# Attention with a gated MLP and a spectral MLP on one core: order of the state scan, the key product and the transposes, and masks read from PSUM

## The chip, the cores and the metric

One core of a Trainium2 chip runs one program. The engines are TensorE (PE; its weight loads are the rows PEld), VectorE (DVE), ScalarE (ACT), GpSimd (POOL) and SyncE (SP, which here only issues transfers). The metric is device time in microseconds (us) of one launch, lower is better; a run of the kernel before and one of the kernel after are compared by their medians.

## The reference

Three blocks follow each other; all of it is fp32.

```
# 1 linear attention with decay: q, k, v, alpha are [4, 8, 768, 48]
for t in range(768):
    state = alpha[:, :, t, :, None] * state + einsum('bhd,bhe->bhde', k[:, :, t], v[:, :, t])
    y[:, :, t] = einsum('bhd,bhde->bhe', q[:, :, t], state)
# 2 gated MLP on x = y as [4, 768, 384]
u, v = split(gelu(x @ w_in), 2)              # d_ff 1024
v = layernorm(v) * g_ln
x = x + (u * (w_sg @ v + b_sg)) @ w_out      # w_sg is [768, 768], over the sequence
# 3 spectral MLP
u = x + real(fft(fft(x, axis=1), axis=2))
out = u + relu(layernorm(u) @ w_ch1) @ w_ch2 # 384 -> 1536 -> 384
```

## The kernel before

**Attention (`attention`, L53 to L295).** The 32 heads are 16 pairs (NG), two heads on 2 x 48 partitions. The sequence is cut into 6 chunks of 128. A pair is a "full step", a half of it (3 chunks) a "half-step" `h`; `g, f = divmod(h, 2)`. Per pair DVE does a backward scan of alpha (`scan1`, L104), a clamp and a reciprocal (L107, L108), the forward scan (`scan2`, L113), the key product (L114, k times the backward scan, in place) and the state scan over chunks (`zscan`, L146). POOL makes the query product (L123). PE makes scores (L154), DVE masks them (L159), and PE makes the output from scores and values (L167, L168) and from queries and states (L173); ACT copies it out (L178 to L181). The keys are transposed by PE (L129), copied by ACT (L131), and multiplied with the values (L141, L142) into the PSUM tile `kp`. Behind `kp`'s 288 columns, in the same tile, lies one column `one` of ones, which both scans read by broadcast. ACT also checks the range of alpha (L119).

**The order.** Every engine does its instructions in the order in which the program writes them; semaphores are set by the framework from the tiles that an instruction reads and writes. The half-steps 2 to 31 are a loop (L263 to L294). An even one starts with `scan1(g + 2)` and then `zscan(g)`, an odd one with `scan2(g + 2)`, which holds the key product, and the query product. Then come scores and mask of the next half-step, one projection unit (`fill(h, 0)`, from half-step 10 on), the transposes (`trk`) of the next pair, the output (`pv`), and at odd half-steps both halves of the key-value product of the next pair (`kv`). Last stands `fill(h, 1)`, two steps of the weight conversion.

**Weight conversion (`Wide`, L419 to L466).** The weights come in as 64-bit numbers. 62 jobs of 128 x 256 or 128 x 192 turn them into fp32 pieces: DVE masks the high word (L438), ACT rescales (L439 to L441), DVE joins sign and body (L446), masks again (L447), and POOL adds and multiplies the low parts (L445, L448, L449). `first` and `second` are the two steps of a job; a third action, `done`, splits the result into a high and a low part (ACT, then POOL, L385 and L388) or stores it. Two steps per half-step convert the input weights and 6 others in the attention, to half-step 20; two of them are `second` of one job and `first` of the next.

**Gated MLP (`gmlp`, L636 to L746).** `proj` runs projection units (L588 to L609) with normalization on DVE and ACT in between, and after each unit two steps of `wsg` (the split of the spatial weight; its low part by POOL or DVE) and one of the weight conversion. `spatial(b)` has 8 units: 18 matmuls with the spatial weight into PSUM, DVE's L700 and L701, ACT's copy L704, DVE's subtraction L707, then the output product `wout` of the unit before, and three conversion steps. `wo_ready` converts ahead of the first four `wout` whatever output weight pieces are still missing.

Of the kernel before, what the change touches and what calls it, by code (L numbers as in the profile page):

```python
# [22 lines left out]
NC = S // CH  # L23
# [29 lines left out]
def attention(tc, st):  # L53
# [22 lines left out]
    qhs = [const(f"qh{i}", [R2, NC, CE]) for i in range(3)]  # L76
    bank = ps_t.tile([R2, 512], F32, name="kp")
    kp, one = bank[:, 0:D * NC].rearrange("p (e c) -> p e c", c=NC), bank[:, D * NC:D * NC + 1]
    ps_u = ctx.enter_context(tc.tile_pool(name="a_psu", bufs=1, space=PSUM, reuse_waits="tile"))
# [21 lines left out]
    def scan1(g, cs=ALL):  # L101
        ak, sf = G[g]["ak"], sfs[g % 3]
        a, z = cs.start * CE, cs.stop * CE
        V.tensor_tensor_scan(out=flat(sf)[:, a:z - 1][:, ::-1], data0=ak[:, a + 2:z + 1][:, ::-1], data1=one.to_broadcast([R2, z - a - 1]), initial=1.0, op0=ALU.mult, op1=ALU.min)  # L104
        V.memset(grid(ak)[:, cs, 0], 0.0)
        p0 = w_p.tile([R2, NC], F32, tag="p0", name="p0")[:, cs]
        V.tensor_scalar(out=p0, in0=sf[:, cs, 0], scalar1=1e-14, scalar2=None, op0=ALU.max)  # L107
        V.reciprocal(out=grid(ak)[:, cs, 1], in_=p0)  # L108

    def scan2(g, cs=ALL):  # L110
        ak, sf, rr = G[g]["ak"], sfs[g % 3], qhs[g % 3]
        j = slice(cs.start * CE, cs.stop * CE)
        V.tensor_tensor_scan(out=flat(rr)[:, j], data0=ak[:, j], data1=one.to_broadcast([R2, j.stop - j.start]), initial=0.0, op0=ALU.mult, op1=ALU.max)  # L113
        V.tensor_tensor(out=sf[:, cs, 1:CE - 1], in0=chunks(ak[:, QK:QK + S])[:, cs], in1=sf[:, cs, 1:CE - 1], op=ALU.mult)  # L114

# [99 lines left out]
    V.memset(kp, 0.0)  # L215
    V.memset(one, 1.0)
    warmup(4)
    NH = 2 * NG
    half = slice(0, 3), slice(3, NC)

    def ready(g, f):
        scan1(g, half[f])
        scan2(g, half[f])
        qhat(g, half[f])

# [31 lines left out]
    scan1(2)  # L257
    zscan(1)
    scan2(2)
    qhat(2)  # L260
    acheck(2)
    load_ak(5)
    for h in range(2, NH):  # L263
        g, f = divmod(h, 2)
        nx, ahead, near = h + 1 < NH, g + 2 < NG, g + 1 < NG
        if ahead and not f:
            load_v(g + 2)
            scan1(g + 2)
            if h > 2:
                zscan(g)  # L270
        if ahead and f:
            scan2(g + 2)
            qhat(g + 2)
            acheck(g + 2)
            if g + 5 < NG:
                load_ak(g + 5)
        if not (ahead or f):
            zscan(g)
        if nx:
            for i in range(3):  # L280
                sc(h + 1, i)
            att(h + 1)
            st["fill"](h, 0)
        if near and h > 2:
            trk(g + 1, f)
        pv(h)
        if h == 2:
            trk(2, 0)
        if near and f:
            kv(g + 1, 0)  # L290
            kv(g + 1, 1)
        if h == NH - 3:
            flag(tc, st, ones[:, 0:2], w_p, ps_t)
        st["fill"](h, 1)  # L294
    ctx.close()  # L295
# [122 lines left out]

class Wide:  # L419
    def __init__(self, nc, pool, w, const, ahead):  # L420
        self.nc, self.pool, self.w, self.const, self.ahead = nc, pool, w, const, ahead
        self.n_done = 0

    def tile(self, n, dt, w, bufs):
        return self.pool.tile([128, self.w], dt, tag=n, name=n, bufs=bufs)[:, 0:w]

    def load(self, job):
# [5 lines left out]
    def first(self, j):  # L433
# [3 lines left out]
        low = j["low"] = j["raw"].bitcast(F32).rearrange("p (a b) -> p a b", b=2)[:, :, 0]  # L437
        nc.vector.tensor_scalar(out=x, in0=j["hi"], scalar1=0x7FFF0000, scalar2=None, op0=ALU.bitwise_and)  # L438
        nc.scalar.activation(mid, h16[:, :, 2], AF.Copy, scale=2.0 ** -20)  # L439
# [3 lines left out]
    def second(self, j):  # L443
        nc, x, mid, hi = self.nc, j["x"], j["mid"], j["hi"]
        nc.gpsimd.tensor_tensor(out=mid, in0=mid, in1=j["low"], op=ALU.add)  # L445
        nc.vector.scalar_tensor_tensor(out=x, in0=hi, scalar=-2 ** 31, in1=x, op0=ALU.bitwise_and, op1=ALU.bitwise_or)  # L446
        nc.vector.tensor_scalar(out=hi, in0=x, scalar1=-2 ** 23, scalar2=None, op0=ALU.bitwise_and)  # L447
        nc.gpsimd.tensor_tensor(out=mid, in0=mid, in1=hi.bitcast(F32), op=ALU.mult)  # L448
# [187 lines left out]
def gmlp(tc, st):  # L636
# [33 lines left out]

    def proj(units, b, n):
        ns = norm(b)
        for i, u in enumerate(units):
            u()
            if i == 1:
                flush()
            take(ns, 1 + (i >= len(units) - n))
            st["gfill"](-1, 1)
        pj.flush()
        for _ in ns:  # L680
            pass
# [7 lines left out]
    def spatial(b):  # L689
        ut = pj.u[b % 2]  # L690
        for h in range(2):
            acc = [None] * KD
            for d in range(KH):
# [30 lines left out]
                if b < 2 and t < NT:  # L724
                    src = st["x"][b + 2][:, t]
                    A.copy(xh[:, t], src)
                    xlag.append(lambda t=t, src=src: V.tensor_tensor(out=xl[:, t], in0=src, in1=xh[:, t].bitcast(F32), op=ALU.subtract))
                st["gfill"](h, 3)
                if b == B - 1:
                    st["fft"](KH * h + d)  # L730

    for _ in pj.early:
        pass
    proj(us(1), 0, 0)
    st["after_u"](0)
    rp = ctx.enter_context(tc.tile_pool(name="g_r", bufs=2, **kw))
    spatial(0)
    proj(vs(2) + us(2), 1, 0)
    spatial(1)
    proj(vs(3), 2, 1)  # L740
    spatial(2)
    proj(us(3), 3, 0)
    st["after_u"](B - 1)
# [340 lines left out]
def network(tc, st, tag, front):  # L1084
# [10 lines left out]
    wd = Wide(nc, pool(in_u, "wide", "left"), WJ, st["bias"], 2)  # L1095
    F = {}
    st["proj"] = Proj(tc, st, pool(in_u, "pj", "left"))
    F["wsg"] = plain_steps(nc, pool(raw, "stg1", "left", 4), wsg_jobs(nc, st), 4, HT)
# [142 lines left out]
```

## Time and profile before

| | |
|---|---|
| three runs | 823.48, 824.86, 825.70 us; median 824.86 |
| the profiled execution | 824.26 us, of which the span shown is 822.5 |
| mean granted clock of TensorE | 0.939 of 2.4 GHz |
| busy, share of the span | PE 763.0 us (93%), PEld 708.5 (86%), DVE 518.2 (63%), ACT 319.8 (39%), POOL 263.9 (32%) |
| stages | attention to 206 us, then the gated MLP, then the spectral MLP |

Shares over the whole span mix stages with different limits; a stage is read by itself. "Clock" is the granted share of full speed: 1.00 is 2.4 GHz, 0.50 is 1.2 GHz. A matmul of fp32 operands appears as more than one PE instruction, so that one pair's key-value product of 10 matmuls is 20 rows. In the timeline a bracket gives the idle time of the engine ahead of an instruction and what ended it.

### The profile page before, as it was taken

What the parts mean: (1) busy time and instruction counts of PE and PEld (TensorE: products, weight loads), DVE (VectorE), ACT (ScalarE), POOL (GpSimd) and SP (SyncE); (2) the same over time, 40 slices, a digit from 0 to 9 for tenths busy, and PEclk for the clock granted to TensorE, in tenths of its full rate; (3) what the DMA queues carried; (4) which work ended last, traced back from release to release, by engine and by line L of the source; (5) the groups of instructions that cost most, each with busy time, mean ns of one, the idle gap of its engine ahead of it and who ended that gap; (6) DMA issues with size and microseconds to landing.
All of it is one profiled execution on the core that took longest, in us unless ns stands there. A gap on an engine that the chain in (4) does not pass through costs nothing.

```text
span 822.5 us, 13577 instructions
## 1 busy us (share of the span) xinstructions
PE 763.0 (93%) x5077; PEld 708.5 (86%) x5077; DVE 518.2 (63%) x1163; ACT 319.8 (39%) x757; POOL 263.9 (32%) x309
## 2 busy tenths in 40 slices
PE   6878888999788989979999999999999999999996
PEld 4656667887787879869999999999999999999996
DVE  6778898875788888886667776327533354424321
ACT  3546565553754464452333435123222222122210
POOL 2356774531587566544033266003000000000000
PEclk7755798999989999989999999999999999999998
DMA  9985758733513333310022032000000000000001
GB/s 232 197 173 127 170 121 189 168 76 71 138 58 90 94 92 100 88 49 29 1 60 59 9 109 77 29 1 30 2 29 2 30 1 1 30 1 29 21 9 33
DMA packets 43597, 58.08 MB, mean 71 GB/s; under 512 B 5473, under 2 KB 34177, under 8 KB 43521
## 3 DMA queue, kind: packets, MB, share of 16 engines
q1 hardware_dynamic: 42944, 56.85, 27.6%
q8 instruction: 42, 0.69, 0.4%
q14 instruction: 35, 0.28, 0.1%
q10 hardware_dynamic: 576, 0.26, 0.1%
HBM read 42.93 MB, written 9.44 MB: 64 GB/s over the span
## 4 chain that ended last, share of the span: by engine, by line


## 5 line engine op out<-in xcount | busy, mean ns | idle before, releaser
L1012 DVE SCALAR_TENSOR_TENSOR hl<-h,hh 128x384 fp32r<-128x384 f32 x96 | 53.4, 556 | 143.3 <-ACT hh L1011 143.2
L1011 ACT ACTIVATE hh<-h 128x384 fp32r<-128x384 f32 x96 | 47.2, 491 | 177.3 <-PE h L416 177.3
L414 PE MATMUL h<-unh,wc 128*128 128x384 f32 x288 | 99.3, 345 | 0.0
L415 PE MATMUL h<-unl,wc 128*128 128x384 f32 x288 | 96.4, 335 | 0.1
L416 PE MATMUL a<-wc,hl 128*128 128x384 f32 x288 | 96.4, 335 | 0.0
L416 PE MATMUL h<-unh,wc 128*128 128x384 f32 x288 | 96.3, 334 | 0.0
L415 PE MATMUL a<-wc,hh 128*128 128x384 f32 x288 | 96.2, 334 | 0.0
L414 PE MATMUL a<-wc,hh 128*128 128x384 f32 x288 | 96.2, 334 | 0.0
L416 PE MATMUL h<-wsg,vl 128*128 128x384 f32 x192 | 66.8, 348 | 5.7 <-DVE vl L668 5.7
L415 PE MATMUL h<-wsg,vh 128*128 128x384 f32 x192 | 66.7, 347 | 4.4 <-POOL wsg L388 4.3
L414 PE MATMUL h<-wsg,vh 128*128 128x384 f32 x192 | 66.7, 347 | 1.4 <-ACT ut L609 1.4
L448 POOL TENSOR_TENSOR wm<-wm,wr 128x192 f32<-128x192 f32 (+1 forms) x62 | 43.0, 694 | 44.4 <-DVE wr L447 42.1
L445 POOL TENSOR_TENSOR wm<-wm,wr 128x192 f32<-128x192 f32 (+1 forms) x62 | 46.5, 750 | 28.1 <-ACT wr L440 28.1
L415 PEld LDWEIGHTS h<-unl,wc 128*128 128x128 f32 x288 | 54.2, 188 | 0.3 <-DVE unl L388 0.3
L416 PEld LDWEIGHTS a<-wc,hl 128*128 128x128 f32 x288 | 54.1, 188 | 0.1
L414 PEld LDWEIGHTS h<-unh,wc 128*128 128x128 f32 x288 | 54.1, 188 | 0.0
L416 PEld LDWEIGHTS h<-unh,wc 128*128 128x128 f32 x288 | 54.1, 188 | 0.0
L414 PEld LDWEIGHTS a<-wc,hh 128*128 128x128 f32 x288 | 54.1, 188 | 0.0
L415 PEld LDWEIGHTS a<-wc,hh 128*128 128x128 f32 x288 | 54.1, 188 | 0.0
L173 PE MATMUL y<-qh,z 48*48 48x128 f32 x320 | 30.6, 329 | 20.9 <-DVE z L146 20.9
L449 POOL TENSOR_TENSOR wm<-wx,wm 128x192 f32<-128x192 f32 (+1 forms) x62 | 47.4, 765 | 4.9
L123 POOL TENSOR_TENSOR qh<-q,qh 112x768 f32<-112x768 f32 (+1 forms) x18 | 37.2, 2068 | 34.2 <-DVE qh L113 26.2
(213 smaller groups left out, 1953.1 us busy)
## 6 DMA issues: line engine op xcount, KB each, us to landing
ak<-in_qa SPq DMA_DIRECT2D x26, 290.4 KB, 4.9
v<-in_v SPq DMA_DIRECT2D x16, 288.0 KB, 4.3
wr<-in_w_d SPq DMA_DIRECT2D x18, 256.0 KB, 2.7
wr<-in_w_d SPq DMA_DIRECT2D x24, 192.0 KB, 2.4
raw<-w_s SPq DMA_DIRECT2D x12, 384.0 KB, 3.2
out<-o SPq DMA_DIRECT2D x24, 192.0 KB, 1.9
q<-in_qa SPq DMA_DIRECT2D x26, 144.0 KB, 5.2
wr<-in_win_d SPq DMA_DIRECT2D x12, 256.0 KB, 4.3
```

The source lines that it names most:

```text
L123: P.tensor_tensor(out=qh, in0=chunks(G[g]["q"])[:, cs], in1=qh, op=ALU.mult)
L173: T.matmul(y[e, i, :], d["z"][e, :, c], qhs[g % 3][e, c, 2:], start=False, stop=True, skip_group_check=True)
L414: T.matmul(out, lh, rh, start=first, stop=False)
L415: T.matmul(out, lh, rl, start=False, stop=False)
L416: T.matmul(out, ll, rh, start=False, stop=last)
L445: nc.gpsimd.tensor_tensor(out=mid, in0=mid, in1=j["low"], op=ALU.add)
L448: nc.gpsimd.tensor_tensor(out=mid, in0=mid, in1=hi.bitcast(F32), op=ALU.mult)
L449: nc.gpsimd.tensor_tensor(out=mid, in0=x.bitcast(F32), in1=mid, op=ALU.add)
L1011: A.activation(hh, p, AF.Relu)
L1012: V.scalar_tensor_tensor(out=hl, in0=p, scalar=0.0, in1=hh.bitcast(F32), op0=ALU.max, op1=ALU.subtract)
```

## The change

The tile `kp` becomes 128 partitions high, and three constant columns join `one` in it: the clamp's bound (1e-14) and the two bit masks. The clamp and, while the attention runs, the masks of the conversion become two-operand instructions that read these columns by broadcast. The key product leaves `scan2` and is issued ahead of its forward scan. The state scan is issued ahead of the backward scan. Transposes come ahead of the projection unit; behind them stand the conversion steps, the unit and the output. The key-value product is issued one half per half-step. In the gated MLP the conversion steps are spread differently: none in the first projection, three and four in turn in the spatial stage.

```diff
@@ -74,8 +74,9 @@
...
     qhs = [const(f"qh{i}", [R2, NC, CE]) for i in range(3)]
-    bank = ps_t.tile([R2, 512], F32, name="kp")
-    kp, one = bank[:, 0:D * NC].rearrange("p (e c) -> p e c", c=NC), bank[:, D * NC:D * NC + 1]
+    full = ps_t.tile([128, 512], F32, name="kp")
+    bank, masks = full[0:R2], [full[:, D * NC + 2 + i:D * NC + 3 + i].bitcast(I32) for i in range(2)]
+    kp, one, tiny = bank[:, 0:D * NC].rearrange("p (e c) -> p e c", c=NC), bank[:, D * NC:D * NC + 1], bank[:, D * NC + 1:D * NC + 2]
     ps_u = ctx.enter_context(tc.tile_pool(name="a_psu", bufs=1, space=PSUM, reuse_waits="tile"))
...
@@ -104,14 +105,17 @@
...
         p0 = w_p.tile([R2, NC], F32, tag="p0", name="p0")[:, cs]
-        V.tensor_scalar(out=p0, in0=sf[:, cs, 0], scalar1=1e-14, scalar2=None, op0=ALU.max)
+        V.tensor_tensor(out=p0, in0=sf[:, cs, 0], in1=tiny.to_broadcast(list(p0.shape)), op=ALU.max)
         V.reciprocal(out=grid(ak)[:, cs, 1], in_=p0)
...
     def scan2(g, cs=ALL):
-        ak, sf, rr = G[g]["ak"], sfs[g % 3], qhs[g % 3]
+        ak, rr = G[g]["ak"], qhs[g % 3]
         j = slice(cs.start * CE, cs.stop * CE)
         V.tensor_tensor_scan(out=flat(rr)[:, j], data0=ak[:, j], data1=one.to_broadcast([R2, j.stop - j.start]), initial=0.0, op0=ALU.mult, op1=ALU.max)
-        V.tensor_tensor(out=sf[:, cs, 1:CE - 1], in0=chunks(ak[:, QK:QK + S])[:, cs], in1=sf[:, cs, 1:CE - 1], op=ALU.mult)
+
+    def khat(g, cs=ALL):
+        ak, sf = G[g]["ak"], sfs[g % 3][:, cs, 1:CE - 1]
+        V.tensor_tensor(out=sf, in0=chunks(ak[:, QK:QK + S])[:, cs], in1=sf, op=ALU.mult)
 
...
@@ -214,6 +218,10 @@
...
     V.memset(one, 1.0)
+    V.memset(tiny, 1e-14)
+    for m, z in zip(masks, Wide.MASKS):
+        V.memset(m, z)
+    st["wide"].masks = masks
     warmup(4)
...
@@ -221,6 +229,7 @@
...
         scan2(g, half[f])
+        khat(g, half[f])
         qhat(g, half[f])
...
@@ -256,6 +265,7 @@
...
     zscan(1)
+    khat(2)
     scan2(2)
...
@@ -265,10 +275,11 @@
...
             load_v(g + 2)
-            scan1(g + 2)
             if h > 2:
                 zscan(g)
+            scan1(g + 2)
         if ahead and f:
+            khat(g + 2)
             scan2(g + 2)
...
@@ -280,18 +291,18 @@
...
             att(h + 1)
-            st["fill"](h, 0)
         if near and h > 2:
             trk(g + 1, f)
+        st["fill"](h, 1)
+        st["fill"](h, 0)
         pv(h)
...
             trk(2, 0)
-        if near and f:
-            kv(g + 1, 0)
-            kv(g + 1, 1)
+        if near:
+            kv(g + 1, f)
         if h == NH - 3:
             flag(tc, st, ones[:, 0:2], w_p, ps_t)
-        st["fill"](h, 1)
+    st["wide"].masks = None
     ctx.close()
...
@@ -417,12 +428,20 @@
...
 class Wide:
+    MASKS = 0x7FFF0000, -2 ** 23
+
     def __init__(self, nc, pool, w, const, ahead):
         self.nc, self.pool, self.w, self.const, self.ahead = nc, pool, w, const, ahead
-        self.n_done = 0
+        self.n_done, self.masks = 0, None
 
...
         return self.pool.tile([128, self.w], dt, tag=n, name=n, bufs=bufs)[:, 0:w]
+
+    def mask(self, out, x, i):
+        if self.masks is None:
+            self.nc.vector.tensor_scalar(out=out, in0=x, scalar1=self.MASKS[i], scalar2=None, op0=ALU.bitwise_and)
+        else:
+            self.nc.vector.tensor_tensor(out=out, in0=x, in1=self.masks[i].to_broadcast(list(x.shape)), op=ALU.bitwise_and)
 
...
@@ -435,7 +454,7 @@
...
         low = j["low"] = j["raw"].bitcast(F32).rearrange("p (a b) -> p a b", b=2)[:, :, 0]
-        nc.vector.tensor_scalar(out=x, in0=j["hi"], scalar1=0x7FFF0000, scalar2=None, op0=ALU.bitwise_and)
+        self.mask(x, j["hi"], 0)
         nc.scalar.activation(mid, h16[:, :, 2], AF.Copy, scale=2.0 ** -20)
...
@@ -444,7 +463,7 @@
...
         nc.vector.scalar_tensor_tensor(out=x, in0=hi, scalar=-2 ** 31, in1=x, op0=ALU.bitwise_and, op1=ALU.bitwise_or)
-        nc.vector.tensor_scalar(out=hi, in0=x, scalar1=-2 ** 23, scalar2=None, op0=ALU.bitwise_and)
+        self.mask(hi, x, 1)
         nc.gpsimd.tensor_tensor(out=mid, in0=mid, in1=hi.bitcast(F32), op=ALU.mult)
...
@@ -668,14 +687,14 @@
...
 
-    def proj(units, b, n):
+    def proj(units, b, n, c):
         ns = norm(b)
...
             take(ns, 1 + (i >= len(units) - n))
-            st["gfill"](-1, 1)
+            st["gfill"](-1, c)
         pj.flush()
...
@@ -725,21 +744,21 @@
...
                     xlag.append(lambda t=t, src=src: V.tensor_tensor(out=xl[:, t], in0=src, in1=xh[:, t].bitcast(F32), op=ALU.subtract))
-                st["gfill"](h, 3)
+                st["gfill"](h, 3 + d % 2)
                 if b == B - 1:
...
         pass
-    proj(us(1), 0, 0)
+    proj(us(1), 0, 0, 0)
     st["after_u"](0)
...
     spatial(0)
-    proj(vs(2) + us(2), 1, 0)
+    proj(vs(2) + us(2), 1, 0, 1)
     spatial(1)
-    proj(vs(3), 2, 1)
+    proj(vs(3), 2, 1, 1)
     spatial(2)
-    proj(us(3), 3, 0)
+    proj(us(3), 3, 0, 1)
     st["after_u"](B - 1)
...
@@ -1094,6 +1113,7 @@
...
     F = {}
+    st["wide"] = wd
     st["proj"] = Proj(tc, st, pool(in_u, "pj", "left"))
...
     first, second, spill = win_jobs(nc, st), wo_jobs(nc, st), spill_jobs(nc, st)
```

## Rows read from the trace of the kernel before

**Rows 1.** Busy time by stage: length, engines with counts, clock, DMA share, GB/s.

```profile
58.00:71.60 13.60, 11.21 (x93) 8.61 (x93) 11.16 (x16) 7.09 (x18) 8.22 (x9) 0.50 0.71 151
...
152.20:206.00 53.80, 53.05 (x587) 43.51 (x588) 37.43 (x66) 27.79 (x67) 16.82 (x13) 1.00 0.41 94
206.00:231.00 25.00, 18.00 (x91) 16.27 (x91) 18.55 (x27) 16.87 (x43) 15.24 (x17) 0.93 0.46 122
...
250.00:282.00 32.00, 27.50 (x142) 24.68 (x141) 27.66 (x56) 11.93 (x30) 22.17 (x26) 1.00 0.36 104
...
400.00:800.00 400.00, 399.85 (x2411) 391.97 (x2410) 199.71 (x575) 116.05 (x255) 54.28 (x58) 1.00 0.09 27
```

**Rows 2.** DVE groups, 30 to 155.1 us: busy, mean ns, idle before.

```profile
L104 DVE TENSOR_TENSOR_SCAN sf<-ak,kp 112x779 f32<-112x779 f32 x10 | 17.7, 1765 | 0.0
...
L447 DVE TENSOR_SCALAR wr<-wx 128x256 int32<-128x256 int32 x18 | 10.9, 606 | 0.6
L438 DVE TENSOR_SCALAR wx<-wr 128x256 int32<-128x256 int32 x18 | 10.3, 570 | 0.0
L446 DVE SCALAR_TENSOR_TENSOR wx<-wr,wx 128x256 int32<-128x256 int32 x18 | 8.4, 464 | 17.5 <-ACT wx L441 17.5
```

**Rows 3.** Single lines, min/median/max ns; then L107's total from 30 to 155.1.

```profile
L438 DVE TENSOR_SCALAR wx<-wr x62: 245/280/1077, 33.8 to 377.0; 128x192 int32<-128x192 int32 x32, 128x256 int32<-128x256 int32 x30
...
L159 DVE TENSOR_TENSOR at<-sp,mask x32: 917/944/958, 9.5 to 199.9; 128x768 f32<-128x768 f32 x32
...
L107 DVE TENSOR_SCALAR p<-sf x18: 161/162/523, 4.7 to 179.6; 112x6 f32<-112x6 f32 x14, 112x3 f32<-112x3 f32 x4
...
30.00:155.10 125.10, 3.69 (x10) 0.75 0.75 162
```

**Rows 4.** DVE's timeline in one full step: start us, length us.

```profile
72.46 0.28 DVE L438 TENSOR_SCALAR wx<-wr 128x256 int32<-128x256 int32 x1
74.46 0.42 DVE L446 SCALAR_TENSOR_TENSOR wx<-wr,wx 128x256 int32<-128x256 int32 x1 [1.71 <-ACT wx L441]
...
77.29 1.43 DVE L114 TENSOR_TENSOR sf<-ak,sf 112x768 f32<-112x768 f32 x1
...
79.51 0.90 DVE L438 TENSOR_SCALAR wx<-wr 128x256 int32<-128x256 int32 x1
80.99 0.42 DVE L446 SCALAR_TENSOR_TENSOR wx<-wr,wx 128x256 int32<-128x256 int32 x1 [0.58 <-ACT wx L441]
...
83.94 0.52 DVE L107 TENSOR_SCALAR p<-sf 112x6 f32<-112x6 f32 x1
```

**Rows 5.** POOL's timeline in the same full step.

```profile
77.86 2.40 POOL L123 TENSOR_TENSOR qh<-q,qh 112x768 f32<-112x768 f32 x1
```

**Rows 6.** ACT's timeline in the same full step.

```profile
72.90 0.48 ACT L178 COPY ys<-y 112x384 f32<-112x384 f32 x1 [4.52 <-PE y L173]
...
73.93 0.50 ACT L441 ACTIVATE wx<-wx,bias 128x256 int32<-128x256 int32 x1
```

**Rows 7.** PE's timeline in the same full step.

```profile
71.75 1.10 PE L173 MATMUL y<-qh,z 48*48 48x128 f32 x8 [2.38 <-DVE z L146]
...
77.86 0.34 PE L141 MATMUL kp<-v,kt 128*64 128x48 f32 x1
...
79.09 1.23 PE L154 MATMUL sp<-qh,sf 48*128 48x128 f32 x8
```

**Rows 8.** Waits, 0 to 210 us: total, times, longest.

```profile
DVE sf L104 <- PE kp L142: 8.8, 3, 3.8
```

**Rows 9.** PE's timeline in the first spatial unit, and POOL's.

```profile
227.54 0.69 PE L415 MATMUL h<-wsg,vh 128*128 128x384 f32 x1 [3.21 <-POOL wsg L388]
...
229.95 0.69 PE L415 MATMUL h<-wsg,vh 128*128 128x384 f32 x1 [1.07 <-POOL wsg L388]
...
226.38 4.50 POOL L388 TENSOR_TENSOR wsg<-raw,wsg 128x384 fp32r<-128x384 f32 x4
```

**Rows 10.** DVE's timeline in the first spatial stage: the start of two units.

```profile
237.29 0.61 DVE L700 SCALAR_TENSOR_TENSOR t<-h,gt,bb 128x384 f32<-128x384 f32 x1
...
243.20 0.60 DVE L700 SCALAR_TENSOR_TENSOR t<-h,gt,bb 128x384 f32<-128x384 f32 x1
```

## The prediction

> **What bounds the kernel now.** I read the busy time by stage first. From 400 to 800 us TensorE (PE) is busy 399.85 of 400 us at full clock, so whatever is gained or lost before 400 us goes whole into the end [rows 1]. The linear attention fills the first 206 us. Its last part, from 152.2 to 206, is PE's again (53.05 of 53.80 us). Between about 30 and 152 PE is not the limit: in the 13.60 us from 58.0 to 71.6 it is busy 11.21 us at a clock of 0.50 (1.2 GHz), and VectorE (DVE) 11.16 us. Which of them sets the pace is read from the DVE groups of 30 to 155.1: the scans, the masks and the products have 0.0 to 0.6 us of idle time ahead of them, and the only DVE instruction that waits is L446, 17.5 us in 18 times, for ScalarE's (ACT) L441 [rows 2]. So DVE paces the attention up to 155 us, by its busy time and by this one wait.
>
> The busy time is longer than the work. L438, a mask of 256 columns, takes 245 ns at least, 1077 at most, and 570 in the mean of this stretch [rows 2, 3]. The timeline shows when: at 79.51 it takes 0.90 us, and GpSimd (POOL) is in its 2.40 us product from 77.86 to 80.26; at 72.46 with POOL idle it takes 0.28 [rows 4, 5]. The clamp L107 goes the same way, 0.16 alone and 0.52 at 83.94 [rows 3, 4]. An instruction with one operand in PSUM does not: L159 stays between 917 and 958 ns in all 32 places [rows 3].
>
> The wait of L446 has a floor of 0.58 us (L438, then L441, then L446 follow each other), seen at 80.99, and is 1.71 in the even half-steps, as at 74.46 [rows 4]. There ACT stood 4.52 us at the copy L178, in front of L441 in its queue, until PE had finished the state products L173; these had waited for the state scan L146, which DVE does only behind the backward scan L104 [rows 6, 7].
>
> **The change part by part, over the 18 jobs of 256 columns in this stretch.**
>
> Masks. 36 instructions take 10.9 + 10.3 = 21.2 us [rows 2]. With the mask read from PSUM the instruction becomes a two-operand one that the trace of before does not have. Bounds: 0.28, as the free mask at 72.46, and 0.90, as the hindered one at 79.51 [rows 4]. I take 0.42, the free L446, which has the same width and two operands. 36 x 0.42 = 15.1, saves 6.1 us. At 0.28 it would save 11.1, at 0.60 (no cure at all) nothing.
>
> The Trainium skill has a rule against this part. In "VectorE: DVE Perf Modes", section "The perf-mode tier table", an fp32 `tensor_scalar` in SBUF runs at 2x and a `tensor_tensor`, or anything with PSUM, at 1x. By that table alone each mask would go from 0.28 to about 0.42 and the sum would lose 36 x 0.14 = 5.0 us instead of gaining 6.1. The slow half of the masks beside POOL (0.90) is why I do not follow it [rows 4, 5].
>
> Clamp. Ten times 3.69 us in all; at 0.17 each 1.7, saves 2.0 us [rows 3].
>
> State scan first. L146 comes before the backward scan (1765 ns) and the clamp, so PE's L173, its copy L178 and ACT's L441 are early, and L446 should wait the floor of 0.58: 17.5 - 18 x 0.58 = 7.1 us saved [rows 2, 4]. What is late next on ACT is the odd half-step, where its range check and two copies stand ahead of L441. I allow 0.5 us in four full steps, 2.0 us, between nothing and the present excess, 1.71 - 0.58 = 1.13 each.
>
> What the change adds. The backward scan has waited three times, 8.8 us, for the key-value product L142, though it reads only the constant column beside it [rows 8]. So the program orders all accesses of that PSUM tile, columns that nobody shares included. The masks now lie in it. In program order the key-value product of a half-step stands behind the masks of the same half-step, and is now issued in every half-step, a half at a time. PE therefore holds it until DVE is through the second mask, and the next scoring products are queued behind it on PE. DVE's first PSUM reader of the next half-step waits for it in turn. A full product (20 PE instructions) took from 77.86 to 79.09, 1.23 us at half clock [rows 7]; the odd half-step's 8 of 20 are 0.5 us, and with about 0.3 for the last one to finish and the handover I price it at 0.8. It is exposed where nothing of DVE lies between mask and state scan: about five full steps (the other four have the batch statistics of a projection unit there), 4.0 us. In the other half-step 12 of 20 are 0.7 + 0.3 us, and the key product, now ahead of scan2, covers it: L114 took 1.43 us at 77.29 [rows 4]. I put 1.0 us for what sticks out. If that cover were gone it would cost 1.0 in each of nine.
>
> Key product, transposes, order of the fills. The key product is the same instruction earlier; its worth is the cover just named. The transposes ahead of the unit move ACT's copy of the transposed keys ahead of a Gelu; in this stretch no wait hangs on it, and after 152 us PE runs without a gap. Of the moved DMA issues only the weight load now stands ahead of the store of the attention output on SP; nobody in the stretch waits for either, cost nothing. If a store were waited for, it could cost one issue, under 1 us per half-step.
>
> Attention: -6.1 - 2.0 - 7.1 + 2.0 + 4.0 + 1.0 = -8.2 us. PE's stretch from 152 us only moves.
>
> First projection and first spatial stage. Between 206 and 231 us PE is idle 25.0 - 18.0 = 7.0 us, 3.21 + 1.07 of it for the low part of the spatial weight, which POOL makes in 4.50 us from 226.38, behind the wide jobs [rows 1, 9]. The change takes all 8 wide steps (4 jobs) out of this projection: worth up to 4.3 us. They come back: the first and the third product with the output weight then find their pieces unconverted, and the conversion is issued behind the high-part copy of the unit before, so PE stands for four links of some 0.6 us (L700 takes 0.61), about 2.5 us, twice. Three more jobs also fall into a stage where DVE is busy 27.66 of 32 us and a unit comes every 243.20 - 237.29 = 5.9 us [rows 1, 10]; a job is about 2 x 0.3 + 0.42 + 0.58 = 1.6 us of DVE. From -4.3 (they hide) to +5.5 (5.0 + 4.8 - 4.3). I take 0, in the middle. The later spatial stages get a few steps more beside a full PE, at nothing.
>
> Sum on the profiled execution: 824.26 - 8.2 = 816.1 us. That execution lies 0.60 below the median of the three runs (824.86), so I forecast 816.7.
>
> **Rivals.** A: the lock step decides. If key product and statistics cover nothing and scoring and ACT come late behind each held product, every one of 18 half-steps pays about 1.15 us (0.8 or 1.0, and a part of ACT's delay) = 20.7 against 15.2 saved: 5.5 slower, 830. It decides from 15.2 / 18 = 0.84 us per half-step. For it: the waits in rows 8, and that the product is now held in every half-step. Against: DVE has 1.43 us of its own work in one of the two. The Trainium skill's rule in "PSUM — Partial Sum Buffer", section "PSUM bank collisions raise a hardware error", asks for semaphores by bank and quadrant and not by address, which gives this rival its ground; the three waits agree with it.
>
> B: masks and clamp stay as long as they are, because POOL hinders the new form too. Then 15.2 loses 8.1, the additions of 7.0 stay, and the time is 824; with the output weight's waits up to 829. Against: L159's narrow spread.
>
> C: more is won. The odd half-steps' ACT delay and the handovers vanish, because PE, less often idle, holds its full clock (it has 1.00 from 152 us, 0.50 in rows 1's step), and the projection gains its 4.3: 824.86 - 15.2 - 4.3 = 805, or 809 with half of the additions.
>
> **How the numbers follow.** Forecast 0.62, A 0.14, B 0.14, C 0.10. The forecast's own cases lie between 811 and 822, by the mask's price and the projection's bounds. A difference under 0.3% (2.5 us) cannot be told from none here. B splits between no change and slower, and the forecast's upper end holds a little of no change: faster 0.70, no change 0.16, slower 0.14. The range from 808 to 827 leaves out most of A and the end of C.
>
> **What would show it.** Right: masks at about 0.42 us each whatever POOL does; L446's wait 0.58 in even half-steps; PE's state products without a wait for L146; the stretch up to the last mask about 8 us shorter; full steps of 12.4 us instead of 13.6. The price: DVE's state scan, and in odd half-steps scan2, waiting for the key-value product, itself waiting for a mask. Wrong: masks over 0.5 us; new waits of more than 0.84 us per half-step; PE stalls on the output weight of more than 5 us around 230 to 250 us, or a stretch after 206 us that is not as long as before within 5 us.

## The result, and the profile after

The changed kernel takes 829.07 us (median of 8 runs, 827.10 to 830.86), the kernel before 824.56 beside it (8 runs). The ratio is 1.0054, 95% interval 1.0038 to 1.0071: slower by 4.5 us, 3.1 to 5.9. The forecast was 816.7. The profiled execution of after took 830.67 us, 1.60 above its median, with a span of 828.9.

Lines of after are some 1 to 20 further down: the backward scan is L105, the clamp L108, the forward scan L114, the key product L118, the key-value product L145 and L146, the state scan L150, the masks L444, ACT's step L460, the join L465, POOL's sums L464, L467 and L468, the low split L399, the gating product L719. First the windows, with columns as in [rows 1]: a full step, the end of the attention, the first projection, the first spatial stage and the long last stretch.

```profile
69.00:81.40 12.40, 11.40 (x97) 8.71 (x95) 9.60 (x17) 7.20 (x19) 8.13 (x9) 0.50 0.75 163
150.00:204.00 54.00, 52.33 (x578) 41.94 (x578) 36.16 (x57) 28.30 (x64) 16.00 (x13) 1.00 0.41 90
205.00:231.00 26.00, 21.64 (x119) 20.52 (x116) 13.91 (x25) 15.00 (x36) 10.12 (x9) 0.93 0.42 103
...
250.00:282.00 32.00, 30.28 (x152) 27.91 (x151) 25.33 (x48) 13.80 (x34) 23.95 (x31) 0.95 0.32 97
...
400.00:800.00 400.00, 399.87 (x2411) 391.92 (x2410) 201.64 (x580) 115.62 (x255) 54.17 (x58) 1.00 0.09 27
```

The last stretch is unchanged, so the loss lies ahead of it. The DVE groups of after from 30 to 152.5 us, the same 18 jobs as [rows 2]:

```profile
L114 DVE TENSOR_TENSOR_SCAN qh<-ak,kp 112x780 f32<-112x780 f32 x10 | 17.7, 1771 | 2.0 <-PE kp L146 1.4 <-POOL wm L467 0.6
...
L465 DVE SCALAR_TENSOR_TENSOR wx<-wr,wx 128x256 int32<-128x256 int32 x18 | 11.2, 620 | 12.9 <-ACT wx L460 12.9
L118 DVE TENSOR_TENSOR sf<-ak,sf 112x768 f32<-112x768 f32 x10 | 10.1, 1007 | 0.0
L444 DVE TENSOR_TENSOR wr<-wx,kp 128x256 int32<-128x256 int32 x18 | 7.6, 422 | 0.6
L444 DVE TENSOR_TENSOR wx<-wr,kp 128x256 int32<-128x256 int32 x18 | 7.3, 408 | 0.0
L150 DVE TENSOR_TENSOR_SCAN z<-kp,pb 112x288 f32<-112x288 f32 x9 | 6.7, 746 | 8.1 <-PE kp L146 8.1
...
L108 DVE TENSOR_TENSOR p<-sf,kp 112x6 f32<-112x6 f32 x10 | 1.5, 153 | 0.5
```

Of before, in the stretch of [rows 2]:

```profile
L113 DVE TENSOR_TENSOR_SCAN qh<-ak,kp 112x780 f32<-112x780 f32 x10 | 17.7, 1766 | 0.0
...
L114 DVE TENSOR_TENSOR sf<-ak,sf 112x768 f32<-112x768 f32 x10 | 12.3, 1234 | 0.0
...
L146 DVE TENSOR_TENSOR_SCAN z<-kp,pb 112x288 f32<-112x288 f32 x9 | 6.4, 716 | 0.0
```

The work did become shorter: masks 21.2 to 14.9, clamp 3.7 to 1.5, and the key product 12.3 to 10.1; the join rose from 8.4 to 11.2, in all -7.9 us. But the state scan and the forward scan, which did not wait in this stretch before, now wait 8.1 and 2.0 us, all but 0.6 of it for the key-value product, against 4.6 saved at the join. That leaves 2.4 us by 152 us. Of the state scan's 8.1 us, 3.9 are five waits of 0.60 to 0.84 us, and 4.15 are a single one, in the step with the first projection unit.

Two marks split the rest: the start of the last mask of scores, which closes DVE's part of the attention, and the time from there to the last gating product, which covers the gated MLP. Before they stand at 199.94 us and 260.77 us, after at 199.65 and 267.56. So the attention gained 0.3 us instead of 8.2, and the gated MLP lost 6.8 where I had put 0. (The sum is 2 us over the ratio's 4.5; the profiled execution of after lies 1.6 above its median, that of before 0.3 below.)

### The profile page after: what moved, and what is told of

Its sections match the earlier page's. It is cut to its first block, busy times and chain, and to the rows that moved or that the text cites. A ratio compares the mean times of both kernels' runs of the same rounds, so it can differ in the third digit from the quotient of the medians.

```text
span 828.9 us, 13575 instructions
## 1 busy us (share of the span) xinstructions
PE 766.2 (92%) x5077; PEld 707.7 (85%) x5077; DVE 509.8 (61%) x1166; ACT 321.3 (39%) x757; POOL 260.7 (31%) x309
## 4 chain that ended last, share of the span: by engine, by line
## 5 line engine op out<-in xcount | busy, mean ns | idle before, releaser
L467 POOL TENSOR_TENSOR wm<-wm,wr 128x192 f32<-128x192 f32 (+1 forms) x62 | 45.3, 731 | 47.1 <-DVE wr L442 29.6
L464 POOL TENSOR_TENSOR wm<-wm,wr 128x192 f32<-128x192 f32 (+1 forms) x62 | 47.1, 759 | 20.8 <-ACT wr L459 20.6
L468 POOL TENSOR_TENSOR wm<-wx,wm 128x192 f32<-128x192 f32 (+1 forms) x62 | 48.6, 784 | 4.9
L465 DVE SCALAR_TENSOR_TENSOR wx<-wr,wx 128x192 int32<-128x192 int32 (+1 forms) x62 | 29.2, 472 | 29.3 <-ACT wx L460 29.3
L460 ACT ACTIVATE wx<-wx,bias 128x192 int32<-128x192 int32 (+1 forms) x62 | 29.8, 480 | 43.1 <-DVE wx L442 27.4
```

The costliest lines, as they stand in the source:

```text
L460: nc.scalar.activation(x, x, AF.Relu, scale=8.0, bias=self.const)
L468: nc.gpsimd.tensor_tensor(out=mid, in0=x.bitcast(F32), in1=mid, op=ALU.add)
```

## The experiments

Each was run beside the kernel before (medians 824.0 to 824.6). The difference is (ratio - 1) x 824.1 us; the marks are those of each kernel's profiled execution, which can lie a few us beside the median (e8's is the slowest of its five).

| | kernel | median us | difference, 95% | last mask | to last gating |
|---|---|---|---|---|---|
| after | the change | 829.07 | +4.5 (3.1 to 5.9) | 199.65 | 267.56 |
| e1 | after, conversion steps moved back | 822.13 | -1.2 (-2.3 to -0.1) | 200.53 | 260.36 |
| e2 | before, only the steps moved | 826.90 | +3.0 (1.9 to 4.0) | 198.74 | 264.85 |
| e3 | e1, constants immediate | 819.96 | -3.8 (-5.0 to -2.5) | 195.68 | 260.15 |
| e4 | before, only constants in PSUM | 818.17 | -5.9 (-7.2 to -4.7) | 194.15 | 260.88 |
| e5 | e1, masks in the transposes' tile | 817.10 | -6.8 (-8.2 to -5.4) | 193.20 | 260.26 |
| e6 | e4 and DVE's new order | 812.38 | -12.2 (-14.3 to -10.1) | 189.79 | 260.08 |
| e7 | e1, product whole | 823.68 | -0.7 (-1.8 to 0.5) | 199.25 | 260.63 |
| e8 | e1, conversion behind the product | 809.27 | -15.0 (-16.6 to -13.4) | 188.86 | 260.68 |
| e9 | e8, steps moved as in after | 816.93 | -7.6 (-8.9 to -6.3) | 187.19 | 266.39 |
| e10 | e8, constants immediate | 816.54 | -7.7 (-9.1 to -6.5) | 193.33 | 259.90 |
| e11 | e8, only the projection freed | 811.15 | -12.7 (-13.9 to -11.5) | 188.51 | 261.75 |
| e12 | e8, ten jobs more in the attention | 807.20 | -16.6 (-18.5 to -14.8) | 194.94 | 249.79 |
| e13 | e1, unit ahead of conversion | 826.63 | +3.6 (2.3 to 4.9) | 201.08 | 260.01 |
| e14 | e13, masks in the transposes' tile | 815.65 | -8.5 (-9.6 to -7.3) | 192.24 | 260.23 |
| e15 | e8, product whole | 813.54 | -10.2 (-11.7 to -8.8) | 189.07 | 261.32 |
| e16 | e8, five jobs more in the attention | 802.30 | -20.6 (-22.3 to -18.9) | 186.86 | 251.24 |

**The parts, e1 to e4.** e1 and e2 separate the moved conversion steps from the attention. e1 undoes them in after, by the two edits here; e2 makes them, the other way round, in the kernel before:

```diff
-                st["gfill"](h, 3 + d % 2)
+                st["gfill"](h, 3)
...
-    proj(us(1), 0, 0, 0)
+    proj(us(1), 0, 0, 1)
```

> The changed kernel with one part undone: the first projection again runs one conversion step per unit, every spatial unit three; attention as changed. Theory 1 (the shift of the conversion into the spatial stages costs, the attention gained nothing): the stretch from 205 us to the end is as before, the total 822 to 823.5, that is 6 to 7 us under the changed kernel and at most 2 us under the kernel before; no PE wait of over 2 us on the output weight's pieces around 231 and 246 us. Theory 2 (the stages behind the attention are slow because the changed attention hands over later or in another order): the total stays at 827 to 830.

> The kernel before with only this part: no conversion steps in the first projection, 3 or 4 per spatial unit; attention as before. Theory 1: 830.5 to 832, 6 to 7 us over the kernel before, with the two PE waits of about 2.2 us on the output weight. Theory 2: 824 to 825.5, since the attention is the old one.

e1 is as theory 1 has it: the stages behind the attention take 260.36 us again, as before. e2 falls between the theories. Its gated MLP lost 4.1 us by the marks, not 6.8; of the 2.7 between, 2.3 lie in the first spatial stage, where TensorE had 1.00 of its clock from 230 us on in e2's trace, and in after's 0.73 from 236 to 242 us and 0.72 from 248 to 254.

e3 is e1 with `tensor_scalar` masks and clamp again, by the edits here; e4 is the kernel before with the PSUM constants alone:

```diff
-        V.tensor_tensor(out=p0, in0=sf[:, cs, 0], in1=tiny.to_broadcast(list(p0.shape)), op=ALU.max)
+        V.tensor_scalar(out=p0, in0=sf[:, cs, 0], scalar1=1e-14, scalar2=None, op0=ALU.max)
...
-    V.memset(tiny, 1e-14)
-    for m, z in zip(masks, Wide.MASKS):
-        V.memset(m, z)
-    st["wide"].masks = masks
```

> The kernel before with only the new order of the attention (key product ahead of the forward scan, state scan first, transposes, conversion and projection unit ahead of the output, key-value product a half at a time); masks and clamp are immediates, the conversion steps lie as before. Theory 1 (PE's key-value product is held by the masks in its PSUM tile, and that eats what the masks save): without the hold the waits of DVE's state scan go from 17 us to under 6, the masks take 21 us again, total 820 to 823. Theory 2 (the new order itself, unit and conversion ahead of output and key-value product, delays the product): the state scan waits as long as in the changed kernel and the masks cost 6 to 8 us more, total 826 to 830.

> The kernel before with only masks and clamp bound read from PSUM; order and conversion steps as before. Theory 1 (two-operand masks are worth 6 to 8 us wherever the key-value product does not stand right behind a mask): here the product is issued once in a full step, ahead of that half-step's second conversion, so attention ends 4 to 8 us earlier and the total is 817 to 821. Theory 2 (the shared PSUM tile costs by itself what the masks save, because the scans ahead wait for the product in any order, or PE sets the pace): 823 to 826.

e4 is as theory 1 has it; e3 lies at the lower end of its theory 1, though its masks take 24.5 us, not 21, and its state scan waits 8.4 us up to 210 us, not under 6. Each alone gains, 3.8 and 5.9 us; together, in e1, they gain 1.2. So the edits work against each other. How shows in a full step of e3, with DVE 11.10 us busy:

```profile
57.40:69.80 12.40, 11.47 (x99) 8.73 (x98) 11.10 (x17) 6.99 (x18) 8.14 (x9) 0.50 0.83 163
```

From one mask of scores to the same one of the next pair it takes 12.37 us (57.33 to 69.70). After takes 12.38 (68.98 to 81.36) with 9.60 us of DVE work: all that the masks gave came back as waiting. The timelines of after, DVE, PE and ACT, in that step (a bracket is the wait ahead, and what ended it):

```profile
71.26 0.42 DVE L444 TENSOR_TENSOR wr<-wx,kp 128x256 int32<-128x256 int32 x1
...
76.88 0.43 DVE L465 SCALAR_TENSOR_TENSOR wx<-wr,wx 128x256 int32<-128x256 int32 x1 [1.24 <-ACT wx L460]
77.34 0.42 DVE L444 TENSOR_TENSOR wr<-wx,kp 128x256 int32<-128x256 int32 x1
78.60 0.76 DVE L150 TENSOR_TENSOR_SCAN z<-kp,pb 112x288 f32<-112x288 f32 x1 [0.83 <-PE kp L146]
```

```profile
71.79 0.31 PE L145 MATMUL kp<-v,kt 128*64 128x48 f32 x1 [0.79 <-ACT ys L182]
...
72.56 1.65 PE L158 MATMUL sp<-qh,sf 48*128 48x128 f32 x12
74.14 0.63 PE L133 MATMUL tp<-ident,sf 112*128 112x112 f32 x2
...
77.91 0.31 PE L145 MATMUL kp<-v,kt 128*64 128x48 f32 x1 [0.21 <-DVE wr L444]
```

```profile
74.81 0.35 ACT L135 COPY kt<-tp 128x224 f32<-128x224 f32 x1 [1.30 <-PE tp L133]
75.06 0.74 ACT L138 COPY pb<-sf 112x288 f32<-112x288 f32 x1
...
76.34 0.51 ACT L460 ACTIVATE wx<-wx,bias 128x256 int32<-128x256 int32 x1
```

Read in order of time: the second mask ends at 71.68, and the held product starts at 71.79 (the bracket names an ACT copy that was done at 71.53; the mask came last). Behind it on PE stand the scores and the transposes; ACT stands at the copy of the transposed keys, with three more instructions between it and the conversion's L460; so the join waits 1.24 us, the next second mask is late, the next product waits for that mask, and the state scan for the product. From the scan it goes by backward scan, mask of scores and first mask to the next second mask: a closed loop over three engines. DVE's waits in the step are 0.57 + 1.24 + 0.83 = 2.64 us, in e3 twice 0.57.

**Which link closes the loop, e5 to e8.**

```diff
# e5, against e1: the masks behind the transposes' 336 columns instead of the product's 290
-    bank, masks = full[0:R2], [full[:, D * NC + 2 + i:D * NC + 3 + i].bitcast(I32) for i in range(2)]
+    bank = full[0:R2]
...
+    tpf = ps_t.tile([128, 512], F32, tag="tp", name="tp")
+    masks = [tpf[:, 3 * R2 + i:3 * R2 + 1 + i].bitcast(I32) for i in range(2)]
# e6: e4 and, of the new order, zscan(g) ahead of scan1(g + 2), khat(g + 2) ahead of scan2(g + 2)
# e7, against e1
-        if near:
-            kv(g + 1, f)
+        if near and f:
+            kv(g + 1, 0)
+            kv(g + 1, 1)
# e8, against e1
-        st["fill"](h, 1)
         st["fill"](h, 0)
         pv(h)
...
             kv(g + 1, f)
+        st["fill"](h, 1)
```

> As e1 (the changed attention, conversion steps of the stages behind it as before), but the two mask constants lie in the PSUM tile of the transposes instead of the key-value product's; the key-value product no longer stands behind a mask of the same tile. Theory 1 (a loop over three engines, second mask, key-value product, scores, transposes, ACT, join, second mask, state scan, sets the 12.4 us of a full step, and the shared tile closes it): the product's holds (0.8 us in the even, 0.2 us in the odd half-step) and the state scan's wait of 0.8 us go, steps of 11.4 to 11.9 us, total 814 to 819. Theory 2 (PE at half clock needs 11.4 us of each 12.4 and paces in any case, or ACT does): steps of 12.2 us or more, total 821 to 824.

> As e4 (masks and clamp bound in PSUM, all else as before), with DVE's part of the new order added: state scan ahead of the backward scan, key product ahead of the forward scan. Unit, transposes, output, conversion and the whole key-value product lie as before. Theory 1 (the state products' wait of 3 to 4 us per full step on the state scan goes, and nothing comes in its place, since the product is issued half a step earlier): 813 to 817, 2 to 5 us under e4. Theory 2 (the state scan first now waits for the key-value product, which stands behind the odd half-step's output): the scan waits over 1.5 us per full step, total 818 to 823, not better than e4.

> As e1, but both halves of the key-value product are issued at odd half-steps, as in the kernel before. Theory 1 (the even half-step's hold behind a mask is one link of the loop): the even hold goes, and all 20 products stand between the odd half-step's second mask and the state scan: the scan's wait grows from 0.8 to about 1.5 us, the step loses about as much as it gains, 821 to 824. Theory 2 (the split itself is the fault): 816 to 820.

> As e1, but the conversion steps stand behind the key-value product again, as in the kernel before (transposes, unit, output, product, conversion). The masks still lie in the product's tile, so now the masks wait for the product and not the product for the masks. Theory 1 (the product held behind the masks closes the loop): the product runs right behind the output, the state scan's wait goes, total 815 to 819. Theory 2 (sharing the tile costs in either order: DVE's first mask waits for PE's product as long as PE waited before): 821 to 826.

e8 moves one line and is 13.8 us under e1 (-15.0 against -1.2), 5.7 below the lower end of its theory 1. Its step from 66.37 to 77.35 takes 10.98 us (second row; the first is the step ahead of it):

```profile
55.40:66.40 11.00, 10.90 (x96) 8.48 (x97) 9.56 (x17) 6.09 (x16) 8.12 (x9) 0.53 0.82 183
66.40:77.40 11.00, 7.98 (x97) 6.23 (x98) 9.70 (x17) 9.08 (x24) 8.55 (x10) 0.84 0.82 186
```

The product on PE, the conversion and the state scan on DVE in it:

```profile
71.92 0.23 PE L145 MATMUL kp<-v,kt 128*64 128x48 f32 x1 [2.22 <-DVE qh L114]
...
77.31 0.23 PE L145 MATMUL kp<-v,kt 128*64 128x48 f32 x1 [0.80 <-ACT ys L182]
```

```profile
73.52 0.70 DVE L465 SCALAR_TENSOR_TENSOR wx<-wr,wx 128x256 int32<-128x256 int32 x1 [0.58 <-ACT wx L460]
74.26 0.42 DVE L444 TENSOR_TENSOR wr<-wx,kp 128x256 int32<-128x256 int32 x1
74.60 0.75 DVE L150 TENSOR_TENSOR_SCAN z<-kp,pb 112x288 f32<-112x288 f32 x1
```

The product is held here too, 2.22 and 0.80 us, longer than in after. But it is released by the scan or clamp ahead (they read columns of its tile), and the state scan comes a mask of scores and a whole conversion later. Its DVE groups from 30 to 146 us show the scan waiting 0.0, and the join 10.8 instead of 12.9; the first masks now wait 2.6, in part for the product, as theory 2 had it:

```profile
L465 DVE SCALAR_TENSOR_TENSOR wx<-wr,wx 128x256 int32<-128x256 int32 x18 | 11.6, 642 | 10.8 <-ACT wx L460 10.8
...
L444 DVE TENSOR_TENSOR wx<-wr,kp 128x256 int32<-128x256 int32 x18 | 7.5, 417 | 2.6 <-PE kp L146 1.4 <-issue 1.0
L150 DVE TENSOR_TENSOR_SCAN z<-kp,pb 112x288 f32<-112x288 f32 x9 | 6.7, 749 | 0.0
```

Nor does the half clock by itself force steps of 12.4 us: the first of the two steps has a clock of 0.53 and takes as long as the second, with PE busy 10.90 of its 11.00 us.

e5 came out at theory 1's total, yet it is no full cure: its constants made PE's transposes wait (0 to 215 us: total, times, longest).

```profile
PE tp L135 <- DVE wr L447: 19.0, 12, 6.6
```

The loop is only a part of the 13.8 us. By the starts of the masks of scores, the three full steps ahead of the first projection unit take 12.4 us each in e1 (12.4, 11.9 and 12.4 in after), but 11.0 each in e5 and 11.3, 11.0 and 11.0 in e8: here the loop decides. The next step, with that unit, takes 15.4 us in e1, 15.5 in after and still 15.3 in e5, against 11.7 in e8 and 14.1 before. No mask holds the product ahead of the state scan there. Of after, DVE, PE and POOL:

```profile
94.11 0.76 DVE L150 TENSOR_TENSOR_SCAN z<-kp,pb 112x288 f32<-112x288 f32 x1 [4.15 <-PE kp L146]
```

```profile
85.70 0.78 PE L425 MATMUL u<-win,xh 128*128 128x512 f32 x1
...
88.30 0.79 PE L427 MATMUL u<-win,xl 128*128 128x512 f32 x1 [1.40 <-POOL xl L399]
...
93.62 0.26 PE L145 MATMUL kp<-v,kt 128*64 128x48 f32 x1
```

```profile
86.56 0.73 POOL L468 TENSOR_TENSOR wm<-wx,wm 128x256 f32<-128x256 f32 x1
87.25 3.11 POOL L399 TENSOR_TENSOR xl<-x,xh 128x384 fp32r<-128x384 f32 x3
```

The unit stands ahead of output and product on PE, and waits for the low part of x, which POOL makes behind the conversion's sums. The product starts with no wait of its own, and the state scan has waited for it all that time. The granted clock of this step is 0.75 in after and 1.00 in e8; its share of the difference is not shown.

e6 beats both its theories slightly; e7 is as theory 1 has it, with waits of the state scan of 1.41 us instead of 0.83.

**What the masks and the moved steps are worth in the good order, e9 to e12.** e9 is e8 with the two edits that e1 undid, e10 e8 with e3's, e11 e8 with `proj(us(1), 0, 0, 0)` alone. e12 lets the attention go on converting:

```diff
-                st["gfill"](h, 3)
+                st["gfill"](h, 2 + (b > 0))
...
-    wide = wd.steps(first + spill[0:6] + second + spill[6:])
+    wide = wd.steps(first + spill[0:16] + second + spill[16:])
...
-    front(lambda n, h: take(wide, n) if wd.n_done < len(first) + 6 else None, F["wsg"])
+    front(lambda n, h: take(wide, n) if wd.n_done < len(first) + 16 else None, F["wsg"])
```

> The changed kernel with one edit undone: the conversion stands behind the key-value product again, as in e8; the conversion steps stay moved from the first projection into the spatial stages, as in the change. Theory 1 (the moved steps cost what they cost ahead of the old attention, in e2): e8 plus 2 to 4 us, 811.5 to 813.5. Theory 2 (they cost as much as between e1 and the changed kernel): e8 plus 6 to 8 us, 815 to 817.

> As e8, but masks and clamp bound are immediates again. Theory 1 (in an order in which VectorE sets the step, a mask read from PSUM is worth the difference of the masks' busy time, some 6 us, and the clamp 2): 815 to 818. Theory 2 (the order alone is worth all of it, the masks nothing): 808 to 811.

> As e8, but no conversion steps in the first projection, while every spatial unit keeps three (half of the moved steps' edit). Theory 1 (the cost of the moved steps is the wait for the output weight's pieces and the jobs that wo_ready then issues, less 4.5 us of earlier spatial weight): e8 plus 0 to 2 us, 809 to 811.5. Theory 2 (it is the later stages, which get the 8 steps that are still owed): e8 plus 4 to 7 us, 813 to 816.

> As e8, but ten more conversion jobs run inside the attention, in the half-steps from 21 on, where PE is busy 53.05 of 53.80 us and VectorE 37.43 us; the first spatial stage then runs two steps per unit instead of three. Theory 1 (steps are free where PE is the bound and cost where VectorE is): the stretch from 152 us does not lengthen, the first spatial stage shortens by 3 to 6 us, total 803 to 807. Theory 2 (the first spatial stage is bound by something else than VectorE's steps): 808 to 811.

e10: the PSUM constants are worth 7.3 us (-7.7 against -15.0). With e1 and e3 this makes a square: conversion behind the product, they gain 7.3; ahead of it, they lose 2.6. e9: the moved steps cost 7.4 us, theory 2. e11 splits them: the freed projection costs 2.3, the fourth step in every other spatial unit the other 5.1. e12 lies at the upper end of theory 1, whose condition fails: it shortens the gated MLP by 10.9 us but ends the attention 6.1 later, where two steps per half-step leave PE 45.83 us of 50 (second row: its first spatial stage, with PE now full):

```profile
150.00:200.00 50.00, 45.83 (x474) 36.40 (x475) 40.22 (x74) 30.98 (x76) 30.81 (x35) 0.97 0.55 134
227.00:260.00 33.00, 32.76 (x181) 31.71 (x180) 28.10 (x52) 14.66 (x39) 19.91 (x29) 0.98 0.22 63
```

**The rest, e13 to e16.** e13 and e14 swap the two fills of e1 and e5, so that the unit stands first; e15 is e8 with e7's edit; e16 is e12 with one step per half-step from 21 on, and `len(first) + 11`.

> As e1 (conversion and projection unit both ahead of the output and the key-value product, masks in the product's tile), but the unit stands ahead of the conversion. Theory 1 (the place of the conversion costs through two things: the product held by its masks, which stays here, and the unit's split of x queued on POOL behind the conversion, which goes): the step with the first unit falls from 15.4 to about 12 us, those ahead of it keep their 12.4, total 817 to 820. Theory 2 (only the shared tile matters): 821 to 824.

> As e13, but the masks lie in the transposes' PSUM tile, as in e5, so that both things go. Theory 1: as good as e8, 808 to 812. Theory 2 (output and key-value product come late behind the conversion whatever the tile and the queue on POOL): 815 to 818, as e5.

> As e8, but both halves of the key-value product at odd half-steps; it differs from e6 only in the transposes ahead of the unit. Theory 1 (the split of the product brings the 3 us between e6 and e8): 811.5 to 814, as e6. Theory 2 (the transposes ahead of the unit bring them): 808 to 810.5, as e8.

> As e12, but from half-step 21 on one conversion step per half-step instead of two (five jobs more than e8 inside the attention, not ten). In e12 the first spatial stage and the projection behind it were 10.8 us shorter and the end of the attention 6.1 us later. Theory 1 (two steps made VectorE and ACT set the pace there, one leaves it to PE): the last mask of scores at 189 to 191 us, total 800 to 804. Theory 2 (each job costs there in proportion): 3 us later, total 805 to 808.

e13 fits neither theory: it is 4.8 us worse than e1. ACT's L460 now stands behind the unit's Gelu, and the join waits 12.0 us between 77 and 150 us against 8.2 in e1; by these rows the loop got a longer link. e14 differs from e5 only in that the unit stands first, and gains 1.7 us over it, as its step with the first unit does (13.6 us against 15.3); it stays 6.5 us behind e8, with the transposes' waits in it (18.4 us). e15 against e8: the split of the product is worth 4.8 us; against e6: the transposes' place nothing that can be told, or a small loss. e16, -20.6 us, ratio 0.9750 (0.9729 to 0.9771), is the fastest of these kernels. One step per half-step leaves the end of the attention to PE:

```profile
141.00:191.00 50.00, 48.88 (x530) 38.98 (x530) 41.03 (x69) 31.74 (x76) 27.36 (x27) 1.00 0.54 130
```

## Why the prediction was wrong

**The gains were right.** Masks: 0.42 forecast, 408 and 422 ns measured, 6.3 us saved of 6.1. Clamp: 2.2 of 2.0. Both together move the time by 7.3 us (e10) of 8.1. In e8, which has every edit of the attention but the conversion's place, the total gain is 15.0 us (13.4 to 16.6); the working had 15.2 ahead of the additions. That the two meet is in part luck: in e8 the join grew by 3.2 us and the first masks wait 2.6, against 2.0 saved at the key product, and none of this stood in the working. (The 245 ns that the working gives as the least time of a mask of 256 columns is that of one of 192; its sum used 0.28.) The table of "VectorE: DVE Perf Modes" in the Trainium skill ("The perf-mode tier table") agrees on a single mask, which went from the 0.28 of a free one to 0.42, though it lists fp32 and these masks are int32; the loss of 5.0 us by it alone did not come, since more than half of the masks had not run free (means of 570 and 606 ns).

**Step that failed, one: the order of the fills at no cost.** I wrote that no wait hangs on the moved transposes, and passed over the conversion that moves ahead of output and product with them. That line is 13.8 us (e1 against e8); 3.9 of it is there without the constants in PSUM (e3 against e10). In after, 4.15 of the 5.8 us that are missing by 152 us (2.4 found of 8.2) are the state scan's one wait in the step with the first unit.

**Step that failed, two: the masks' gain and the held product as separate terms.** The size of the hold was right where it was priced: I took 4.0 us in five full steps and 1.0 ahead of the forward scan, and the state scan waited 3.9 us in five, the forward scan 1.4. The full step of 12.4 us came out as well (12.4, 11.9, 12.4), but that is luck: e3, without the constants, has the same 12.4, and with the loop open the step is 11.0 (e5, e8). In the step shown, DVE's savings of 1.5 us (11.10 to 9.60) turned into 1.5 us of waits (1.14 to 2.64). In e8 the same product is held up to 2.22 us, and the state scan waits for nothing in that stretch. So the price is not the hold, but what stands between the release and the next reader, and what PE and ACT have queued behind the hold; here that led back to the mask that ends the hold. Rival A had the lock step, at 1.15 us per half-step, but as a price beside the masks' gain; what the runs show is a loop in which that gain is not seen at all. The time came out at A's 830 and at the upper end of B (829), but by neither: the attention did not get slower, as A needs, the masks did get shorter, which B denies, and 6.8 us arose behind the attention. The rule of "PSUM — Partial Sum Buffer" in the Trainium skill ("PSUM bank collisions raise a hardware error") asks for semaphores by bank and not by address. The traces agree in that instructions on different columns of one tile wait for each other, the transposes of e5 and e14 included.

**Step that failed, three: DVE's lead taken for PE's.** I let PE's stretch from 152 us only move. DVE reached that mask of scores 2.3 us sooner than before (149.84), but the last one only 0.3 sooner. PE did not keep that lead: after, it stands in front of the held product, and its next scores begin 0.1 us sooner than before (of before, then of after):

```profile
152.93 0.94 PE L154 MATMUL sp<-qh,sf 48*128 48x128 f32 x12
```

```profile
152.39 0.23 PE L145 MATMUL kp<-v,kt 128*64 128x48 f32 x1 [1.05 <-ACT ys L182]
...
152.84 0.94 PE L158 MATMUL sp<-qh,sf 48*128 48x128 f32 x12
```

(By the bracket an ACT copy ends that wait; the second mask, until 152.29, ended last.) e3, which holds nothing there, reaches that mask of scores 4.27 us sooner than before and the last one still 4.26.

**Step that failed, four: the stages behind the attention at 0 and "at nothing".** By the marks, the first gating product came 4.25 us sooner after the last mask, as the bound of -4.3 had it. The two waits for the output weight came as well, 2.5 us each with the 0.34 and 0.32 that follow:

```profile
233.86 0.44 PE L425 MATMUL a<-gh,wo 128*128 128x384 f32 x1 [2.20 <-ACT wo L396]
...
248.13 0.44 PE L425 MATMUL a<-gh,wo 128*128 128x384 f32 x1 [2.23 <-ACT wo L396]
```

They and the added jobs made the first spatial stage 46.84 us from first to last gating product instead of 40.72 (45.63 in e11, which only frees the projection). So the first part is +1.9, inside its bounds. The second spatial stage, which I had put at nothing beside a full PE, grew from 33.97 to 37.58, and the projections on both sides of it by 1.0 and 1.4: 6.0 us (what follows is 1.1 shorter). With four steps in every other unit PE is not full there any more, 34.61 us of 37.58 against 33.40 of 33.97 (the stage in before, then in after):

```profile
305.90:339.87 33.97, 33.40 (x189) 32.47 (x188) 29.08 (x61) 16.51 (x45) 21.07 (x31) 1.00 0.34 100
```

```profile
308.48:346.06 37.58, 34.61 (x192) 32.97 (x191) 32.10 (x67) 17.93 (x49) 24.64 (x37) 1.00 0.36 100
```

e9 against e11 shows 5.1 us for the same edit, and this stage at 37.44 against 34.58.

## What to carry to other kernels

A held instruction is priced by following what is queued behind it on its engine until a chain ends or comes back to the thing that holds it; if it comes back, the loop's length is the step, and work saved on one engine in it is not seen (here 12.4 us with and without 1.5 us of DVE's work, 11.0 with the loop open). A constant put into a PSUM tile that PE writes ties every reader of the constant to PE: write PE's product where the next work of the reader is something else. Filler work goes to the stage where its engine has slack, and in doses (five jobs gained 5.6 us over e8, ten only 1.6).

## What the runs showed that I had not expected

The contention with POOL did not vanish, it moved. The join, with two operands in SBUF, had a mean of 464 ns before and 620 after, 642 in e8; in e8 it takes 1.13 us beside POOL's split of x (DVE, then POOL):

```profile
79.17 1.13 DVE L465 SCALAR_TENSOR_TENSOR wx<-wr,wx 128x256 int32<-128x256 int32 x1 [0.58 <-ACT wx L460]
```

```profile
77.09 2.93 POOL L399 TENSOR_TENSOR xl<-x,xh 128x384 fp32r<-128x384 f32 x3
```

The rule in "SBUF — State Buffer" of the Trainium skill ("Who interferes with whom"), that a VectorE instruction with two SBUF inputs contends with a GpSimd instruction that reads SBUF, agrees with the 1.13 us; the masks with one operand in PSUM stay at 0.41 and 0.42 beside it. In the four full steps behind the first unit, up to 150 us, this took the gain away: the 16 masks saved 1.3 us, the 8 joins took 2.5 more, and the steps lasted 53.0 us in after and 52.9 before.

What stays open: why the moved steps cost 3.0 us ahead of the old attention (e2) and 5.7 to 7.4 ahead of the new one. The clock of the first spatial stage differs between the traces, but no run here forced it. No run keeps the constants in a PSUM tile that PE never writes, so what the two-operand masks are worth without any tie to PE is not shown.
